# Low parts of g and of the weights on GpSimd, one scaling power for two ff tiles, w_in and w_out handled apart

## The chip, the cores and the metric

The kernel runs on one core of a Trainium2 chip. The metric is the device time of one execution in microseconds. A core has a matrix engine (TensorE, PE in the profile; its weight loads stand apart as PEld), a vector engine (VectorE, DVE), a scalar engine (ScalarE, ACT), GpSimd (POOL) and a sequencer that here issues all transfers (SyncE, SP). Each engine runs its own instructions in order; between engines, semaphores hold an instruction until what it reads is there and what it overwrites is no longer needed. SBUF is the working memory of 128 partitions; PSUM takes the matrix engine's results.

## The reference

Attention within chunks of 64 tokens, then a feed-forward layer with g(h) = h - tanh(h) between its two products. Queries, keys, values and the result are float32, the weights float64.

```python
scores = scale * np.matmul(q_c, k_c.transpose(0, 1, 2, 4, 3))   # chunks of 64, 8 batches, 8 heads
attn = np.exp(scores - np.max(scores, axis=-1, keepdims=True))
attn = attn / (np.sum(attn, axis=-1, keepdims=True) + 1e-09)
out = np.matmul(attn, v_c)
...
x = out.transpose(0, 2, 1, 3).reshape(4608, 512)
h = x @ w_in            # w_in: 512 x 2048
g = h - np.tanh(h)
return (g @ w_out).astype(np.float32)    # w_out: 2048 x 512
```

The weights come to the kernel as 64-bit words and are narrowed on the chip.

## The kernel before

**Tiling.** 4608 tokens are 36 token tiles of 128 (each a pair of chunks, called pair in the code); they go in ten groups of 4, 3, 4, 4, 4, 4, 4, 4, 3 and 2 tiles. The feed-forward layer runs group by group over 16 ff tiles of 128 columns. For one ff tile of one group, `gemm1` (L436) makes h in PSUM (`ph`), `shrink` makes g from it, and `gemm2` (L457) adds g times w_out to one PSUM bank per token tile (`po`). `gemm2` runs two ff tiles behind `gemm1` (`LAG`).

**Splitting.** A product in about float32's precision is made of three products of narrower operands: high times high, low times high, high times low. x and w_in are split into float16 parts (`xh`, `xl`, `wih`, `wil`), g and w_out into parts for the matrix engine's fp32r form (`gh`, `gl`, `woh`, `wol`). For the float16 parts the operands are first scaled by a power of two: `spread` (L94, ACT, sums of magnitudes per partition), the maximum over the partitions (L101, POOL) and three small DVE instructions (L107 to L109) give `to_w` for a tile of w_in or `to_x` for a group's x; `undo` (L422) multiplies the inverse factors, and `shrink` uses that product.

**One unit of the feed-forward layer outside PE:** tanh on ACT (L444), h - tanh on DVE (L445, from PSUM), the high part on ACT (L448), the low part gl on DVE (L449).

**A weight tile** (128 ff columns): SP loads w_in's half (L129, in four blocks) and w_out's half (L127) into one `raw` tile, three of which exist. The 64-bit words are narrowed by one ACT instruction (L139) and three on DVE (L140 shift, L144 merge of the low words, L145 sign), on both halves in one 1024-wide pass or on each half apart. Then w_in's half: spread, power, high part `wih` on ACT (L152), low part `wil` on DVE (L158); w_out's half: high part `woh` on ACT (L154), low part `wol` on DVE (L160).

**Order.** In the first stage, before and during group 0, the attention of the first seven pairs (class Early), the 16 weight tiles and group 0's feed-forward layer run interleaved. The string `PLAN` gives that order by tokens: a and v load a pair's queries, keys and values, l a weight half (l3.1 is w_out's half of tile 3), p the power of x, S M E N n T V the steps of attention, F fill matmuls without use, c a conversion, g `gemm1` and `shrink` of an ff tile (g2.1 for the second two token tiles), h a `gemm2`. Up to the bar SP and PE follow it literally; behind it a planner ranks all engines' instructions by it. Z releases the first stage's tiles, and the parts of weight tiles 8 to 15 are written where these lay. From group 1 on, the attention of the next group (class Late) is spread over the steps of the current one; its DVE instructions L316, L329, L331, L352, L359 and L366 have both inputs in SBUF, L346 and L383 one of them in PSUM.

POOL does the maximum over the partitions, and in the first stage some zero fills (L188, L290).

Of the kernel before, what the change touches and what calls it, by code (L numbers as in the profile page):

```python
# [11 lines left out]
F32 = mybir.dt.float32  # L12
# [23 lines left out]
MOST = max(SIZES) * P  # L36
LAG = 2
RAW = 3
WS = 2
EARLY_FC = 8  # L40
TINY = 2.0 ** -100
EXPONENT = 0x7F800000
# [4 lines left out]
LATE = (-1, 6, 2, 3, 3, 5, 6, 10, 10, 15)  # L47
VALS = (0, 4)
PLAN = """
a0 a1 l0.0 l0.1 a2 v2 F4 F1 v0 F4 S0 v1 v3 p0 l1.0 S1 l1.1 F1 c0 F1 a3 F6 l2.0 c1 F1 E0 N0 T0 S2 F4 l3.0 M1 M2 n1 T1 N2 V0 V1 F7 S3 T2 g0.0 M3 V2 l2.1 N3 T3 V3 | g1.0 c2 l3.1 a4 l4.0 l4.1 v4 g0.1 h c3.0 Y S4 l5.0 g2.0 a6 g3.0 E4 c3.1 h n4 a5 l5.1 c4.1 h l6.0 c4.0 l7.0 g2.1 h g3.1 v6 l6.1 h l7.1 c5 S5 E5 g1.1 g4 S6 E6 h N5 c7.0 n6 g7 c6.0 l8.0 v5 p1 T4 h T5 l8.1 V5 c7.1 c6.1 g6 T6 V4 l9.0 h V6 Z l10.0 h c8 l11.0 h l11.1 l10.1 l9.1 g5 c9 g8 g9 c10.0 h c10.1 l12.0 c11 h l13.0 l12.1 c12 g10 l14.0 h h c13.0 g11 l14.1 l15.0 h g12 l13.1 l15.1 c13.1 g13 h h c14.0 c14.1 c15 h g14 g15 h h  # L50
"""

@with_exitstack
def attn_ffn_kernel(ctx: ExitStack, tc: tile.TileContext, qE, kE, vE, qT, kT, vP, w_in, w_out, out):

# [14 lines left out]
    ps_a = ctx.enter_context(tc.tile_pool(name="ps_a", bufs=2, space=PSUM))  # L70


    wi = [[None, None] for _ in range(FC)]
    wo = [[None, None] for _ in range(FC)]

    def weight_tiles(pool, fcs):
        for fc in fcs:
            for i, a in enumerate("hl"):
                wi[fc][i] = pool.tile([P, DM], F16, name=f"wi{a}{fc}")
# [4 lines left out]
    to_w = const.tile([P, FC], F32, name="to_w")  # L84
    from_w = const.tile([P, FC], F32, name="from_w")

    def new_x():
        return tuple(xpool.tile([P, KC, MOST], F16, name=f"x{a}") for a in "hl")
# [1 line left out]
    def spread(pool, a, out):  # L90

        junk = pool.tile([P, 4 * P * 2], BF16, name="junk", bufs=1)
        n = a.shape[1]
        nc.scalar.activation(junk[:, :n], a, AF.Abs, scale=2.0 ** -10, accum_out=out)  # L94
# [20 lines left out]
        return to, back  # L115


    raws, ws, from_x = {}, {}, {}
    BOTH = slice(0, 2)

    def load_weights(pool, fc, half):
        fs = slice(fc * P, (fc + 1) * P)
        if half == 0:
            raws[fc] = pool.tile([P, 2, DM, 2], U32, name="raw", bufs=RAW)
        raw = raws[fc][:, half]
        if half:
            nc.sync.dma_start(out=raw, in_=w_out[fs])  # L127
        else:
            nc.sync.dma_start(  # L129
                out=raw.rearrange("p (kc f) two -> p kc f two", kc=KC),  # L130
                in_=w_in[:, fs, :].rearrange("(kc p) f two -> p kc f two", p=P),
            )

    def magnitude(pool, fc, part):
        up = raws[fc][:, part, :, 1]
        if fc not in ws:
            ws[fc] = pool.tile([P, 2, DM], U32, name="w", bufs=WS)
        w = ws[fc][:, part]
        nc.scalar.activation(w.bitcast(F32), up.bitcast(F32), AF.Abs, scale=2.0 ** -112)  # L139
        nc.vector.tensor_single_scalar(w, w, 3, op=ALU.logical_shift_left)  # L140

    def narrow(pool, fc, part):
        low, up, w = raws[fc][:, part, :, 0], raws[fc][:, part, :, 1], ws[fc][:, part]
        nc.vector.scalar_tensor_tensor(out=w, in0=low, scalar=29, in1=w, op0=ALU.logical_shift_right, op1=ALU.bitwise_or)  # L144
        nc.vector.scalar_tensor_tensor(out=w, in0=up, scalar=0x80000000, in1=w, op0=ALU.bitwise_and, op1=ALU.bitwise_or)  # L145
        if part in (0, BOTH):
            w = ws[fc][:, 0].bitcast(F32)
            sums = pool.tile([P, 1], F32, name="wsum", bufs=2)
            spread(pool, w, sums)
            to, back = to_w[:, fc:fc + 1], from_w[:, fc:fc + 1]  # L150
            power(pool, "w", sums, to, back)
            nc.scalar.activation(wi[fc][0], w, AF.Copy, scale=to)  # L152
        if part in (1, BOTH):
            nc.scalar.copy(out=wo[fc][0], in_=ws[fc][:, 1].bitcast(F32))  # L154

    def rest(fc, part):
        if part in (0, BOTH):
            nc.vector.scalar_tensor_tensor(out=wi[fc][1], in0=ws[fc][:, 0].bitcast(F32), scalar=to_w[:, fc:fc + 1], in1=wi[fc][0], op0=ALU.mult, op1=ALU.subtract)  # L158
        if part in (1, BOTH):
            nc.vector.tensor_sub(wo[fc][1], ws[fc][:, 1].bitcast(F32), wo[fc][0])  # L160

    def weights(pool, fc, part=BOTH):
        magnitude(pool, fc, part)
        narrow(pool, fc, part)
        rest(fc, part)


    def transposed(pool, psum, s):
# [240 lines left out]
    class FeedForward:  # L409
# [2 lines left out]

        def __init__(self, g, x):
            self.g, self.x, self.queue, self.po = g, x, [], []
            self.sig, self.known = const.tile([P, FC], F32, name="sig", bufs=2), set()

        def undo(self, fc):

            if fc not in self.known:
                some = {fc} if self.g == 0 else set(range(FC))  # L420
                fs = slice(min(some), max(some) + 1)
                nc.vector.tensor_scalar_mul(self.sig[:, fs], from_w[:, fs], from_x[self.g])  # L422
                self.known |= some
            return self.sig[:, fc:fc + 1]

        def room(self, pool, tiles):
            self.po += [pool.tile([P, DM], F32, name=f"po{t}") for t in tiles]
# [1 line left out]
        def gemm1(self, fc, t0, t1):  # L429
            cols, n = slice(t0 * P, t1 * P), (t1 - t0) * P  # L430
            x = self.x
            ph = ps_h.tile([P, MOST], F32, name="ph")[:, :n]
            k = 0
            for a, b in ((0, 0), (1, 0), (0, 1)):
                for kc in range(KC):
                    nc.tensor.matmul(ph, lhsT=wi[fc][a][:, kc * P:(kc + 1) * P], rhs=x[b][:, kc, cols], start=(k == 0), stop=(k == 3 * KC - 1))  # L436
                    k += 1
            self.ph = fc, t0, t1, n, ph

        def shrink(self):  # L440
            fc, t0, t1, n, ph = self.ph
            t = ffn.tile([P, MOST], F32, name="t", bufs=3)[:, :n]
            sig = self.undo(fc)
            nc.scalar.activation(t, ph, AF.Tanh, scale=sig)  # L444
            nc.vector.scalar_tensor_tensor(out=t, in0=ph, scalar=sig, in1=t, op0=ALU.mult, op1=ALU.subtract)  # L445
            gh = ffn.tile([P, MOST], F32R, name="gh")[:, :n]
            gl = ffn.tile([P, MOST], F32R, name="gl")[:, :n]
            nc.scalar.copy(out=gh, in_=t)  # L448
            nc.vector.tensor_sub(gl, t, gh)  # L449
            self.queue.append((fc, t0, t1, (gh, gl)))  # L450

        def gemm2(self):
# [52 lines left out]
    def step(token):  # L505

        nonlocal first_psum
        kind, n, part = re.fullmatch(r"([a-zA-Z])(\d*)\.?(\d*)", token).groups()
        n, part = int(n or 0), int(part) if part else None
        if kind == "l":  # L510
            load_weights(raw, n, part)
        elif kind == "a":
            att.load(n)
        elif kind == "v":
            att.load_values(n)
        elif kind == "p":
            from_x[n] = att.powers(range(FIRST[n], FIRST[n + 1]))
        elif kind == "F":
            for _ in range(n):
                nc.tensor.matmul(idle, lhsT=warm[:, :P], rhs=warm, start=True, stop=True)  # L520
        elif kind == "S":
            att.scores(n)
        elif kind in "ME":
            att.largest(n)
            att.exponents(n, summed=kind == "E")
        elif kind in "Nn":
            att.sums(n)
            att.normalise(n, by_head=kind == "n")
        elif kind == "T":
            att.transpose(n)  # L530
            att.weights(n)
        elif kind == "V":
            att.values(n)
            att.result(n, *((x, n) if n < SIZES[0] else (nx, n - SIZES[0])))
        elif kind == "c":
            weights(raw, n, BOTH if part is None else part)
# [76 lines left out]
```

## Time and profile before

| | us |
|---|---|
| median of three runs | 902.7 (901.23 to 904.43) |
| the profiled execution | 903.85 |
| its span in the profile | 902.1 |
| PE busy / DVE / ACT / POOL in the span | 879.1 / 635.0 / 510.5 / 20.4 |

Times in profile rows are microseconds from the span's start, unless a mean is in ns. A row of the timeline reads: start, duration, engine, line, operation, written tile <- read tiles, shapes, count, and in brackets the idle time before it and what ended that. A row of a group reads: line, engine, operation, tiles, shapes, count | busy us, mean ns of one | idle time before them and what ended it. A row of the chain reads: start, duration, engine, tile, line, count. The chain is followed back from the last instruction, at each step to what released it. Spans on POOL are rough, and a matmul's end is modelled, so that neighbouring matmul records overlap.

### The profile page before, as it was taken

How to read it: one execution, taken by the hardware profiler on the slowest of the kernel's cores; microseconds unless marked ns; L12 is line 12 of the kernel's file. 1: busy time of each engine (PE TensorE's matmuls, PEld its weight loads, DVE VectorE, ACT ScalarE, POOL GpSimd, SP SyncE). 2: the span in 40 equal slices, each digit the busy share in tenths (PEclk: the TensorE clock that was granted, in tenths of full speed). 3: DMA queues.
4: the chain of work that ended last, by engine and by line, in shares of the span. 5: the costliest groups of instructions: out<-in, count | busy, mean ns of one | idle time of the engine just before them, and what ended most of it. 6: DMA issues, size and time to landing. Idle time of an engine off the chain costs nothing.

```text
span 902.1 us, 13875 instructions
## 1 busy us (share of the span) xinstructions
PE 879.1 (97%) x4905; PEld 596.5 (66%) x4905; DVE 635.0 (70%) x1331; ACT 510.5 (57%) x1109; POOL 20.4 (2%) x44
## 2 busy tenths in 40 slices
PE   8899979999999999999999999999999999999998
PEld 6776546676566666666666666666666666677776
DVE  5896897988677767785778576857785567447332
ACT  6697666775655555555565555556564455344232
POOL 2000011000000000000000000000000000000000
PEclk8798999999999999999999999999999999999999
DMA  9772243343332322232222232323232122101100
GB/s 232 207 226 93 95 163 115 108 105 80 102 77 60 93 86 79 71 82 94 82 71 76 84 82 69 90 82 82 71 84 81 39 66 60 59 24 25 47 1 24
DMA packets 78453, 78.25 MB, mean 87 GB/s; under 512 B 36912, under 2 KB 52272, under 8 KB 78384
## 3 DMA queue, kind: packets, MB, share of 16 engines
q1 hardware_dynamic: 78384, 77.36, 30.3%
q8 instruction: 39, 0.64, 0.3%
q14 instruction: 30, 0.25, 0.1%
HBM read 60.29 MB, written 9.44 MB: 77 GB/s over the span
## 4 chain that ended last, share of the span: by engine, by line
PE 80%; DVE 8%; ACT 4%; DMA 4%; issue 2%; SPq 1%; POOL 0%; ACTq 0%; DVEq 0%
PE po L457 38%; PE ph L436 36%; PE psa L341 3%; PE psa L379 2%; PE psa L271 1%; DVE t L445 1%; ACT junk L94 1%; DVE w L144 1%; DMA raw<-w_out 1%; DMA vr<-vP 1%; DMA k<-kE 1%; DVE v16l L316 1%; DVE w L145 1%; DVE gl L449 1%; ACT t L444 1%
## 5 line engine op out<-in xcount | busy, mean ns | idle before, releaser
L457 PE MATMUL po<-woh,gh 128*128 128x512 f32 x576 | 239.4, 416 | 0.9 <-ACT gh L448 0.9
L457 PE MATMUL po<-woh,gl 128*128 128x512 f32 x576 | 227.2, 396 | 0.6 <-DVE gl L449 0.5
L457 PE MATMUL po<-wol,gh 128*128 128x512 f32 x576 | 226.0, 392 | 0.0
L436 PEld LDWEIGHTS <-wih 128*128 128x128 f16 x1312 | 117.2, 99 | 129.5 <-issue 27.3
L445 DVE SCALAR_TENSOR_TENSOR t<-ph,sig,t 128x512 f32<-128x512 f32 (+2 forms) x164 | 112.3, 685 | 111.9 <-ACT t L444 109.3
L444 ACT ACTIVATE t<-ph,sig 128x512 f32<-128x512 f32 (+2 forms) x164 | 104.2, 636 | 136.9 <-PE ph L436 127.1
L436 PE MATMUL ph<-xh,wih 128*128 128x512 f16 (+2 forms) x656 | 155.5, 361 | 8.8 <-ACT wih L152 5.2
L436 PE MATMUL ph<-xh,wil 128*128 128x512 f16 (+2 forms) x656 | 153.8, 358 | 0.7 <-DVE wil L158 0.7
L436 PE MATMUL ph<-xl,wih 128*128 128x512 f16 (+2 forms) x656 | 152.7, 356 | 0.1
L449 DVE TENSOR_TENSOR gl<-t,gh 128x512 fp32r<-128x512 f32 (+2 forms) x164 | 102.5, 625 | 64.9 <-ACT gh L448 62.4
L448 ACT CAST gh<-t 128x512 fp32r<-128x512 f32 (+2 forms) x164 | 92.6, 565 | 81.5 <-PE po L457 60.8
L457 PEld LDWEIGHTS po<-woh,gl 128*128 128x128 f32 x576 | 108.2, 188 | 27.1 <-DVE gl L449 2.9
L457 PEld LDWEIGHTS po<-woh,gh 128*128 128x128 f32 x576 | 108.8, 189 | 24.9 <-ACT gh L448 2.4
L457 PEld LDWEIGHTS po<-wol,gh 128*128 128x128 f32 x576 | 108.8, 189 | 19.0
L436 PEld LDWEIGHTS <-wil 128*128 128x128 f16 x656 | 64.3, 99 | 63.8 <-DVE wil L158 2.4
L345 ACT COPY slo<-psa 64x128 f32<-64x128 f32 x232 | 59.4, 256 | 56.6 <-DVE s L346 54.3
L346 DVE TENSOR_TENSOR s<-psa,slo 64x128 f32<-64x128 f32 x232 | 66.1, 285 | 15.6 <-ACT slo L345 12.1
L316 DVE SCALAR_TENSOR_TENSOR v16l<-vr,to_x,v16h 64x256 f16<-64x256 f32 x116 | 52.3, 478 | 19.6 <-ACT v16h L314 18.4
L341 PE MATMUL psa<-ks,qs 128*128 128x256 f32 x232 | 57.0, 326 | 2.9 <-DVE ks L331 2.7
L341 PEld LDWEIGHTS psa<-ks,qs 128*128 128x128 f32 x232 | 43.0, 189 | 17.5 <-PE ph L436 2.5
L314 ACT ACTIVATE v16h<-vr,to_x 64x512 f16<-64x512 f32 x58 | 41.7, 719 | 16.4 <-PE psa L379 15.6
L329 DVE TENSOR_TENSOR qs<-qr,qs 64x512 fp32r<-64x512 f32 x58 | 39.7, 685 | 2.4 <-ACT qs L328 1.5
(81 smaller groups left out, 762.4 us busy)
## 6 DMA issues: line engine op xcount, KB each, us to landing
qr<-qT SPq DMA_DIRECT2D x116, 128.0 KB, 2.7
kr<-kT SPq DMA_DIRECT2D x116, 128.0 KB, 2.7
out<-t SPq DMA_DIRECT2D x36, 256.0 KB, 2.3
raw<-w_in SPq DMA_DIRECT2D x16, 512.0 KB, 4.1
raw<-w_out SPq DMA_DIRECT2D x16, 512.0 KB, 5.2
vr<-vP SPq DMA_DIRECT2D x58, 128.0 KB, 2.6
qbd<-qE SPq DMA_DIRECT2D x14, 128.0 KB, 4.8
k<-kE SPq DMA_DIRECT2D x7, 256.0 KB, 5.1
```

The lines of the kernel that those rows point to most:

```text
L314: nc.scalar.activation(vh[r, :, :, r], v[r], AF.Copy, scale=to[r])
L316: nc.vector.scalar_tensor_tensor(out=vl[r, c, :, r], in0=v[r, c], scalar=to[r], in1=vh[r, c, :, r], op0=ALU.mult, op1=ALU.subtract)
L329: nc.vector.tensor_sub(qs[D:], qr[D:], qs[D:])
L341: nc.tensor.matmul(ps[:, i], lhsT=d["qs"][:, h, :], rhs=d["ks"][:, h], start=True, stop=True)
L345: nc.scalar.copy(out=slo[r], in_=ps[r, :, 1, r])
L346: nc.vector.tensor_add(d["s"][r, 2 * j:2 * j + 2, :], ps[r, :, 0, r], slo[r])
L436: nc.tensor.matmul(ph, lhsT=wi[fc][a][:, kc * P:(kc + 1) * P], rhs=x[b][:, kc, cols], start=(k == 0), stop=(k == 3 * KC - 1))
L444: nc.scalar.activation(t, ph, AF.Tanh, scale=sig)
L445: nc.vector.scalar_tensor_tensor(out=t, in0=ph, scalar=sig, in1=t, op0=ALU.mult, op1=ALU.subtract)
L448: nc.scalar.copy(out=gh, in_=t)
L449: nc.vector.tensor_sub(gl, t, gh)
L457: nc.tensor.matmul(self.po[t], lhsT=gg[a][:, ts], rhs=wo[fc][b], start=(fc == 0 and i == 0), stop=(fc == FC - 1 and i == 2))
```

## The change

- gl of every unit (L449) moves from DVE to POOL.
- Of weight tiles 2 to 15, w_out's low part moves to POOL; w_in is scaled in place on POOL, its high part is a plain ACT copy of that, and its low part a POOL subtraction. Tiles 0 and 1 stay on ACT and DVE.
- One power serves two neighbouring ff tiles: `to_w`, `from_w` and `sig` have 8 columns in place of 16; the reduction takes two columns, and one small DVE maximum is added.
- w_in and w_out have raw tiles and conversions of their own: two raw tiles for pairs of w_in tiles, three for w_out; every narrowing pass is 512 wide. w_in is laid out on the host so that a tile is one contiguous block.
- PLAN is written anew for this.

```diff
-a0 a1 l0.0 l0.1 a2 v2 F4 F1 v0 F4 S0 v1 v3 p0 l1.0 S1 l1.1 F1 c0 F1 a3 F6 l2.0 c1 F1 E0 N0 T0 S2 F4 l3.0 M1 M2 n1 T1 N2 V0 V1 F7 S3 T2 g0.0 M3 V2 l2.1 N3 T3 V3 | g1.0 c2 l3.1 a4 l4.0 l4.1 v4 g0.1 h c3.0 Y S4 l5.0 g2.0 a6 g3.0 E4 c3.1 h n4 a5 l5.1 c4.1 h l6.0 c4.0 l7.0 g2.1 h g3.1 v6 l6.1 h l7.1 c5 S5 E5 g1.1 g4 S6 E6 h N5 c7.0 n6 g7 c6.0 l8.0 v5 p1 T4 h T5 l8.1 V5 c7.1 c6.1 g6 T6 V4 l9.0 h V6 Z l10.0 h c8 l11.0 h l11.1 l10.1 l9.1 g5 c9 g8 g9 c10.0 h c10.1 l12.0 c11 h l13.0 l12.1 c12 g10 l14.0 h h c13.0 g11 l14.1 l15.0 h g12 l13.1 l15.1 c13.1 g13 h h c14.0 c14.1 c15 h g14 g15 h h
+a0 a1 l0.0 l1.0 v0 v1 a2 v2 v3 p0 F4 F1 l0.1 F4 S0 S1 l1.1 F1 a3 F6 l2.0 l3.0 E0 c0.0 c1.0 N0 T0 S2 F4 M1 M2 n1 c0.1 T1 N2 V0 V1 F7 S3 T2 l2.1 g0.0 c1.1 M3 V2 l3.1 N3 T3 V3 | g1.0 c2.0 c3.0 a4 l4.0 l5.0 v4 g0.1 h c2.1 Y S4 l4.1 l5.1 g1.1 a6 g2.0 E4 c3.1 h n4 a5 c4.0 c5.0 h l6.0 l7.0 c4.1 g3.0 h v6 g2.1 h l6.1 l7.1 c5.1 S5 E5 g3.1 h g4 S6 E6 h N5 c6.0 c7.0 n6 g5 l8.0 l9.0 v5 p1 T4 h T5 c6.1 V5 c7.1 g6 T6 V4 h V6 Z l8.1 l9.1 c8.0 c9.0 l10.0 l11.0 g7 h c8.1 g8 c9.1 h g9 l10.1 l11.1 c10.0 c11.0 h c10.1 l12.0 l13.0 c11.1 l12.1 c12.0 c13.0 g10 l13.1 h c12.1 g11 l14.0 l15.0 h g12 c13.1 l14.1 l15.1 c14.0 c15.0 h g13 c14.1 c15.1 h g14 h g15 h h h
...
         if half:
-            nc.sync.dma_start(out=raw, in_=w_out[fs])
...
+            raw_out[fc] = pool.tile([P, DM, 2], U32, name="raw_out", bufs=RAW)
+            nc.sync.dma_start(out=raw_out[fc], in_=w_out[fc])
+            return
+        j, i = divmod(fc, 2)
+        if i == 0:
+            raw_in[j] = pool.tile([P, 2, DM, 2], U32, name="raw_in", bufs=2)
+        nc.sync.dma_start(out=raw_in[j][:, i], in_=w_in[fc])
+
+    def merged(w, raw):
+        low, up = raw[:, :, 0], raw[:, :, 1]
         nc.scalar.activation(w.bitcast(F32), up.bitcast(F32), AF.Abs, scale=2.0 ** -112)
         nc.vector.tensor_single_scalar(w, w, 3, op=ALU.logical_shift_left)
...
         nc.vector.scalar_tensor_tensor(out=w, in0=low, scalar=29, in1=w, op0=ALU.logical_shift_right, op1=ALU.bitwise_or)
         nc.vector.scalar_tensor_tensor(out=w, in0=up, scalar=0x80000000, in1=w, op0=ALU.bitwise_and, op1=ALU.bitwise_or)
...
+    def weights(pool, fc, part):
+        if part:
+            w = pool.tile([P, DM], U32, name="w_out", bufs=2)
+            merged(w, raw_out.pop(fc))
+            w = w.bitcast(F32)
+            nc.scalar.copy(out=wo[fc][0], in_=w)
+            (nc.vector if fc < 2 else nc.gpsimd).tensor_sub(wo[fc][1], w, wo[fc][0])
+            return
+        j, i = divmod(fc, 2)
+        if i == 0:
+            w_in_f[j] = pool.tile([P, 2, DM], U32, name="w_in", bufs=2), pool.tile([P, 2], F32, name="wsum", bufs=2)
+        w, sums = w_in_f[j]
+        merged(w[:, i], raw_in[j][:, i])
+        w = w.bitcast(F32)
+        spread(pool, w[:, i], sums[:, i:i + 1])
+        if i == 0:
+            return
+        to = to_w[:, j:j + 1]
+        power(pool, "w", sums, to, from_w[:, j:j + 1])
+        h, l = wi[j]
+        for i in range(2):
+            if j == 0:
+                nc.scalar.activation(h[:, i], w[:, i], AF.Copy, scale=to)
+                nc.vector.scalar_tensor_tensor(out=l[:, i], in0=w[:, i], scalar=to, in1=h[:, i], op0=ALU.mult, op1=ALU.subtract)
+            else:
+                nc.gpsimd.tensor_scalar_mul(w[:, i], w[:, i], to)
+                nc.scalar.copy(out=h[:, i], in_=w[:, i])
+                nc.gpsimd.tensor_sub(l[:, i], w[:, i], h[:, i])
...
-            nc.vector.tensor_sub(gl, t, gh)
+            nc.gpsimd.tensor_sub(gl, t, gh)
...
-        "w_in": bits(inputs["moe_w_in"]),
+        "w_in": bits(inputs["moe_w_in"].reshape(KC, P, FC, P).transpose(2, 1, 0, 3)),
```

More of the change, by code (lines that the diff above doesn't have):

```diff
@@ L70, in attn_ffn_kernel @@
     ps_a = ctx.enter_context(tc.tile_pool(name="ps_a", bufs=2, space=PSUM))
-    wi = [[None, None] for _ in range(FC)]
+    wi = [[None, None] for _ in range(FC // 2)]
     wo = [[None, None] for _ in range(FC)]
@@ L78, in weight_tiles @@
             for i, a in enumerate("hl"):
-                wi[fc][i] = pool.tile([P, DM], F16, name=f"wi{a}{fc}")
+                if fc % 2 == 0:
+                    wi[fc // 2][i] = pool.tile([P, 2, DM], F16, name=f"wi{a}{fc // 2}")
                 wo[fc][i] = pool.tile([P, DM], F32R, name=f"wo{a}{fc}")
     weight_tiles(const, range(EARLY_FC))
-    to_w = const.tile([P, FC], F32, name="to_w")
-    from_w = const.tile([P, FC], F32, name="from_w")
+    to_w = const.tile([P, FC // 2], F32, name="to_w")
+    from_w = const.tile([P, FC // 2], F32, name="from_w")
     def new_x():
@@ L115, in token_power @@
         return to, back
-    raws, ws, from_x = {}, {}, {}
-    BOTH = slice(0, 2)
+    raw_in, raw_out, w_in_f, from_x = {}, {}, {}, {}
     def load_weights(pool, fc, half):
[L122 to L125, printed above, removed]
         if half:
-            nc.sync.dma_start(out=raw, in_=w_out[fs])
[L128 to L132, printed above, removed]
@@ L414, in __init__ @@
             self.g, self.x, self.queue, self.po = g, x, [], []
-            self.sig, self.known = const.tile([P, FC], F32, name="sig", bufs=2), set()
+            self.sig, self.known = const.tile([P, FC // 2], F32, name="sig", bufs=2), set()
         def undo(self, fc):
[L419 to L422, printed above, removed]
+            j = fc // 2
+            if j not in self.known:
+                some = {j} if self.g == 0 else set(range(FC // 2))
+                js = slice(min(some), max(some) + 1)
+                nc.vector.tensor_scalar_mul(self.sig[:, js], from_w[:, js], from_x[self.g])
                 self.known |= some
-            return self.sig[:, fc:fc + 1]
+            return self.sig[:, j:j + 1]
         def room(self, pool, tiles):
@@ L535, in step @@
         elif kind == "c":
-            weights(raw, n, BOTH if part is None else part)
+            for k in (0, 1) if part is None else (part,):
+                weights(raw, n, k)
         elif kind == "g":
@@ L605 @@
         if a.dtype == np.int64:
-            ap = ap.bitcast(U32).rearrange("a (b two) -> a b two", two=2)
+            ap = ap.bitcast(U32).rearrange("a b (c two) -> a b c two", two=2)
         args.append(ap)
```

30 lines of the change are left out of this document (2 added, 28 removed).

## The prediction

> **What bounds the kernel now.** I read the page's first two parts first.
>
> ```profile
> PE 879.1 (97%) x4905; PEld 596.5 (66%) x4905; DVE 635.0 (70%) x1331; ACT 510.5 (57%) x1109; POOL 20.4 (2%) x44
> PEclk8798999999999999999999999999999999999999
> ```
>
> PE is busy nearly everywhere and POOL hardly ever; the granted clock is under nine tenths only in three of the first four slices. A busy PE row counts overlapping records, so it does not say whether PE runs at its pace. For that I took the table by windows (columns: PE, PEld, DVE, ACT, POOL, clock, DMA share, GB/s) and the chain in order of time.
>
> ```profile
> 60.00:80.00 20.00, 18.80 (x106) 12.92 (x103) 16.39 (x49) 19.32 (x67) 1.43 (x4) 1.00 0.27 93
> 100.00:120.00 20.00, 15.54 (x67) 8.32 (x65) 18.85 (x37) 12.45 (x22) 2.29 (x3) 1.00 0.46 158
> 120.00:139.40 19.40, 18.21 (x75) 10.76 (x75) 18.79 (x42) 13.93 (x27) 1.05 (x3) 0.91 0.25 82
> 240.00:850.00 610.00, 609.92 (x3383) 406.79 (x3382) 424.48 (x872) 327.09 (x682) 3.47 (x6) 1.00 0.26 71
> ...
> 242.36 2.61 PE ph L436 x12
> 244.97 2.76 PE po L457 x12
> ```
>
> From 240 to 850 us PE has no gap, and the chain is PE alone: 2.61 + 2.76 = 5.37 us for one ff tile of four token tiles. Nothing on DVE, ACT or POOL can shorten that stretch. Between 100 and 139.4 us it is DVE that is full (37.64 of 39.4 us, 96%). From 60 to 80 it is ACT (19.32 of 20), so relief of DVE buys little there.
>
> What DVE's load costs PE is read from the power of each weight tile, one POOL reduction per tile. The first and the last of the eight in the second half of the weights, and the matmul that waited longest:
>
> ```profile
> 97.32 0.35 POOL L101 PARTITION_ALL_REDUCE wall<-wsum  x1 [18.24 <-ACT junk L94]
> 139.67 0.55 POOL L101 PARTITION_ALL_REDUCE wall<-wsum  x1 [5.97 <-ACT junk L94]
> 120.91 1.89 PE L436 MATMUL ph<-xh,wih 128*128 128x512 f16 x4 [4.63 <-ACT wih L152]
> ```
>
> Seven distances in 139.67 - 97.32 = 42.35 us: a weight tile comes every **6.05 us**, while PE would use one every 5.37. The 0.68 us between them, seven times, is 4.8 us; the 4.63 us gap is most of it in one place. This stretch decides the change.
>
> **The change there, part by part.** DVE's groups in the stretch from 97 to 140 us, seven tiles' worth:
>
> ```profile
> L158 DVE SCALAR_TENSOR_TENSOR wil<-w,to_w,wih 128x512 f16<-128x512 f32 x7 | 5.2, 748 | 0.0
> L445 DVE SCALAR_TENSOR_TENSOR t<-ph,sig,t 128x512 f32<-128x512 f32 x7 | 5.2, 744 | 1.2 <-ACT t L444 1.2
> L144 DVE SCALAR_TENSOR_TENSOR w<-raw,w 128x1024 uint32<-128x1024 uint32 x4 | 4.9, 1222 | 0.0
> L145 DVE SCALAR_TENSOR_TENSOR w<-raw,w 128x1024 uint32<-128x1024 uint32 x4 | 4.9, 1218 | 0.0
> L449 DVE TENSOR_TENSOR gl<-t,gh 128x512 fp32r<-128x512 f32 x7 | 4.8, 684 | 0.0
> L160 DVE TENSOR_TENSOR wol<-w,woh 128x512 fp32r<-128x512 f32 x7 | 4.8, 683 | 0.0
> L144 DVE SCALAR_TENSOR_TENSOR w<-raw,w 128x512 uint32<-128x512 uint32 x6 | 4.0, 689 | 0.1
> L145 DVE SCALAR_TENSOR_TENSOR w<-raw,w 128x512 uint32<-128x512 uint32 x6 | 4.0, 686 | 0.0
> L140 DVE TENSOR_SCALAR w<-w 128x512 uint32<-128x512 uint32 x6 | 2.5, 424 | 0.0
> L140 DVE TENSOR_SCALAR w<-w 128x1024 uint32<-128x1024 uint32 x3 | 2.1, 691 | 0.0
> L422 DVE TENSOR_SCALAR sig<-from_w,from_x 128x1 f32<-128x1 f32 x6 | 1.2, 203 | 0.0
> L109 DVE RECIPROCAL to_w<-from_w 128x1 f32<-128x1 f32 x7 | 1.1, 158 | 0.1
> L107 DVE TENSOR_SCALAR wall<-wall 128x1 uint32<-128x1 uint32 x7 | 1.1, 154 | 1.8 <-POOL wall L101 1.8
> L108 DVE TENSOR_SCALAR from_w<-wall 128x1 f32<-128x1 f32 x7 | 1.0, 148 | 0.1
> ```
>
> They add up to 46.8 us, 6.69 per tile; set against 6.05, an instruction overlaps its neighbour so that 0.905 of its duration counts.
>
> DVE loses L158, L160 and L449 (0.748 + 0.683 + 0.684 = 2.12 us) and half of the power and of sig. It pays for the split of the halves: two 512-wide passes, 2 x (0.424 + 0.689 + 0.686) = 3.60 us, where the joint form took 0.691 + 1.222 + 1.218 = 3.13. The power of a pair has one more small reduction (taken as 0.154, like L107): (0.158 + 0.154 + 0.148 + 0.154) / 2 = 0.31. With sig 0.10 and L445 0.744 that is 4.75, times 0.905 = **4.30 us** of DVE's own work per tile, below PE's 5.37. Were DVE alone to decide, PE would set the pace: -0.68 x 7 = -4.8 us.
>
> POOL gets three subtractions (low parts of g, w_in, w_out; price X each), one scaling (price Y) and half a reduction (0.18 of the 0.35). The trace holds no POOL instruction with two inputs. The nearest row is a pass of 512 columns that only writes:
>
> ```profile
> L188 POOL MEMSET qbd<- 64x512 f32 x4 | 2.1, 520 | 0.2
> ```
>
> X is at least one such pass, 0.52, and at most three, one after the other, 1.56. I take two, **X = 1.04**, since two operands have to come in; Y = 0.52, one operand (at most 1.04, which would add 0.52 x 7 = 3.6 us). POOL's own load is then 3 x 1.04 + 0.52 + 0.18 = 3.82 us per tile, under 5.37: POOL alone sets no pace.
>
> **What POOL and DVE do to each other** is the open price. Three pairs from the timeline, POOL's reduction and the DVE instruction that was running when it began:
>
> ```profile
> 115.98 1.23 DVE L144 SCALAR_TENSOR_TENSOR w<-raw,w 128x1024 uint32<-128x1024 uint32 x1
> 116.07 1.34 POOL L101 PARTITION_ALL_REDUCE wall<-wsum  x1 [7.27 <-ACT junk L94]
> ...
> 107.90 0.68 DVE L449 TENSOR_TENSOR gl<-t,gh 128x512 fp32r<-128x512 f32 x1
> 108.20 0.60 POOL L101 PARTITION_ALL_REDUCE wall<-wsum  x1 [5.43 <-ACT junk L94]
> ...
> 133.05 0.75 DVE L445 SCALAR_TENSOR_TENSOR t<-ph,sig,t 128x512 f32<-128x512 f32 x1
> 133.35 0.35 POOL L101 PARTITION_ALL_REDUCE wall<-wsum  x1 [5.71 <-ACT junk L94]
> ```
>
> Beside L445, which has one operand in PSUM, the reduction takes 0.35 us. Beside L144 it takes 1.34 and ends 0.20 after it (117.41 against 117.21); beside L449 it takes 0.60 and ends 0.22 after it. Both have two SBUF inputs: POOL stood until DVE was through. That DVE stands while POOL reads is not shown. Either DVE does not, and the pace is PE's, or it does, and the two engines' instructions of this sort follow one another.
>
> In the second case DVE's merge passes (L140, L144, L145), 3.60 x 0.905 = 3.26 us per tile, and POOL's 3.82 share one lane: 7.08 us per tile, 1.03 more than now, times 7: **+7.2 us**. At X = 0.52 it is 5.52 per tile, -3.7 us; at X = 1.56 it is 8.64, +18.1 us. It breaks even at X = (6.05 - 3.26 - 0.70) / 3 = 0.70. I take the second case, because the one direction that is seen is a full stand and not a slowdown, and because 7.08 is further from 6.05 than a little overlap takes away. I count L140 in the lane: 512 more columns cost it 0.267 us, L144 0.533, so it draws two columns at once.
>
> The Trainium skill, "SBUF — State Buffer", section "Who interferes with whom", states that a VectorE instruction with two SBUF inputs and a GpSimd instruction that reads SBUF hold one shared pair of ports in turn, each for its whole length, whichever starts first; the POOL side of it agrees with the 1.34 us above, and the other side no row here shows. Its page "GPSIMD Engine Reference", section "Elementwise — side-by-side cycle accounting", gives 4497 ns for an add of 2048 columns; a quarter, 1.12 us (an estimate), in place of 1.04 would make the lane 7.32 and the term +8.9.
>
> **The other parts.** Start: the first real matmul waits for x, whose power came from POOL at 26.34.
>
> ```profile
> 26.34 0.38 POOL L101 PARTITION_ALL_REDUCE xall<-vsum  x1 [5.98 <-ACT junk L94]
> 28.90 1.01 PE L436 MATMUL ph<-xh,wih 128*128 128x256 f16 x4 [2.00 <-ACT xh L278]
> ```
>
> The new order puts the same bytes ahead of the last value tile (w_in of tile 1 where w_out of tile 0 was), and ACT's work ahead of x stays about even: one more spread and one more wih, one woh and the joint L139 of tile 1 less. Tile 1's weights are then there with tile 0's, which saves a later wait, but the conversions of w_out move behind it. -1 us, between -3 and +2.
>
> The transfers: w_in becomes one block per tile, and raw tiles are kept apart.
>
> ```profile
> SPq L129 <- DVE w L145: 74.5, 12, 18.3
> ```
>
> SP's loads of w_in wait for a free raw tile, 74.5 us in sum, so a load that lands faster is behind that wait: 0. SP gets no more transfers of weights, and what stands behind a waiting load on SP (values and keys of the next group) waits on the same merges as now.
>
> Groups 1 and 2: here DVE prepares attention ahead, and PE lacks a little.
>
> ```profile
> 160.00:180.00 20.00, 18.52 (x100) 13.01 (x98) 19.03 (x42) 14.68 (x35) 0.00 (x0) 1.00 0.41 115
> 220.00:240.00 20.00, 18.03 (x103) 10.91 (x101) 13.37 (x30) 12.50 (x27) 0.00 (x0) 1.00 0.27 79
> ```
>
> PE lacks 1.48 + 1.97 = 3.5 us in these two. DVE loses sixteen subtractions of 384 columns, at three quarters of 0.684 some 8.2 us; in the lane POOL's sixteen (0.78 each, 12.5 us) give back what meets a two-input DVE instruction, about half. -2 us, between -4 (all of the gap and a little more) and +3 (all of the 12.5 given back).
>
> Steady groups: gl takes X + up to one DVE instruction (1.7 us) in place of 0.68 and is read two ff tiles later, 2 x 5.37 us; the cover is PE's own work, so 0. Were the cover gone, 0.36 us a tile would show. In POOL's order the subtraction of w_in's low part waits for ACT's copy; the next gl and the next power stand behind it, and PE's second product behind gl: within the same two tiles. Tail: the chain's last product run (18 matmuls, three ff tiles), and the last gl.
>
> ```profile
> 895.36 0.42 DVE L449 TENSOR_TENSOR gl<-t,gh 128x256 fp32r<-128x256 f32 x1 [0.60 <-ACT gh L448]
> ...
> 893.73 4.12 PE po L457 x18
> ```
>
> The last ff tile's third begins 2.75 us into that run, at 896.48; its gl was done at 895.78 and may come 0.70 later, more than a 256-wide POOL pass adds (half of 1.04 against 0.42). 0.
>
> **Sum**, against the profiled execution (903.85 us, its span 902.1): +7.2 - 1 - 2 = +4.2, so 908.0 there. The median of the three runs, 902.7, is 1.15 below that execution; for the median I say **906.9**.
>
> **The rivals.**
> *DVE never stands for POOL (faster).* It decides if POOL's hold on the lane costs DVE under 1.75 us a tile (6.05 - 4.30). For it: only POOL is seen to stand, DVE drops from 6.05 to 4.30. Against: the full stand of 1.34. Price: -4.8 - 1 - 4 = -9.8, 892.9; some 2.5 us more if the stretch at half clock (84.52, twelve matmuls in 5.07 us in place of 2.61) goes too.
>
> ```profile
> 84.52 5.07 PE ph L436 x12
> ```
>
> *POOL is dear.* X near 1.56: +18.1 - 1 + 3 = +20.1, 922.8. For it: no two-input row at all; against: a pass that writes 0.52 is quick.
> *The lane fills, but earlier work pays.* Before 97.32 POOL sat 18.24 us and DVE was not full; if the in-halves of one pair are merged in that hole, 2 x 1.80 x 0.905 = 3.3 us leave the stretch: +4.2 - 3.3 = +0.9, 903.6, no change. Against: its raw tiles come free late.
>
> **How the numbers follow.** Chances: forecast 0.42 (own range 901 to 913), no standing 0.35, dear POOL 0.10, paid earlier 0.13. A measurement of this kernel tells about 0.3% (2.7 us) from no change. Slower: 0.28 of the forecast's 0.42, all 0.10, 0.03 of the fourth: 0.41. Same: 0.11 + 0.02 + 0.08 = 0.21. Faster: 0.03 + 0.33 + 0.02 = 0.38. Range **888 to 916**: it takes in the case without standing with part of its 2.5, and stops short of dear POOL.
>
> **What would show it.** In the changed profile: DVE instructions with two SBUF inputs that last over a microsecond or idle behind POOL, and a spacing of pairs near 2 x 7.1 us between 97 us and the end of the weights, would show the lane; two-input DVE rows unchanged at 0.68 beside POOL's, and pairs every 10.7 us, would show it wrong. POOL's row of gl gives X. Past 240 us the chain should stay PE's at 5.37 a tile; if not, the cover was wrong and so is the sum.

## The result and the profile after

| | before | after |
|---|---|---|
| median, us | 902.16 (901.23 to 904.43) | 1022.74 (1020.40 to 1024.72) |
| ratio | | 1.1331 (1.1293 to 1.1370) |
| span of the profiled execution | 902.1 | 1022.8 |

The change costs 120.6 us. A small loss was forecast, 4.2 us; the sign is as forecast, the size is nearly thirty times the forecast's. The profile's page of after, first two parts:

```profile
PE 919.0 (90%) x4903; PEld 608.6 (60%) x4903; DVE 578.4 (57%) x1142; ACT 512.5 (50%) x1118; POOL 267.9 (26%) x242
...
PEclk9876957779999999999999999999999999999999
```

DVE's busy time fell by 56.6 us, as the change meant it to, and no engine looks like the bound: POOL, the only one whose share of the span grew, is at 26%. The low clock digits now reach to the ninth slice (230 us) instead of the fourth. So the page says where to look, and not why. Here are windows of after in that stretch (columns as in the prediction: PE, PEld, DVE, ACT, POOL, clock, DMA share, GB/s):

```profile
140.00:160.00 20.00, 9.19 (x29) 3.55 (x28) 6.86 (x13) 5.04 (x9) 9.68 (x7) 0.66 0.07 20
160.00:180.00 20.00, 7.28 (x21) 3.16 (x20) 5.88 (x12) 5.71 (x12) 9.87 (x9) 0.68 0.10 35
...
240.00:850.00 610.00, 586.25 (x3204) 383.36 (x3202) 398.69 (x790) 332.63 (x703) 137.66 (x111) 0.99 0.28 78
```

In these 40 us of the first stage nobody is busy: PE under half, DVE a third, POOL half, and the granted clock is at 0.66 and 0.68. Past 240 us, where its first stage ends, PE lacks 23.75 of 610 us. Before it lacked 0.08 of these, and 4.2 of the 88.5 us from its own stage's end (151.5) to 240. Both halves of the forecast are therefore to be explained, the first stage and the "0" of the steady groups.

How much belongs to which half is read from the transfers of the result: group 0's first one marks the end of the first stage, the last one the end of the work. The groups of transfers, of before and of after (last two numbers: first and last start):

```profile
L484 SPq DMA_DIRECT2D out<-t x36: 332/344/1541, 151.5 to 898.6; - x36
```

```profile
L484 SPq DMA_DIRECT2D out<-t x36: 332/344/1667, 240.9 to 1019.8; - x36
```

The first stage takes 89.4 us more, all that follows 31.8 more (778.9 against 747.1).

What everybody waits for is seen on POOL's timeline in that stage. One full pair of w_in tiles of after, and the reduction that opens the next:

```profile
139.37 0.37 POOL L101 PARTITION_ALL_REDUCE wall<-wsum  x1 [5.76 <-issue]
147.15 1.25 POOL L449 TENSOR_TENSOR gl<-t,gh 128x512 fp32r<-128x512 f32 x1 [7.40 <-issue]
148.40 3.12 POOL L162 TENSOR_SCALAR w_in<-w_in,to_w 128x512 f32<-128x512 f32 x2
151.50 1.25 POOL L143 TENSOR_TENSOR wol<-w_out,woh 128x512 fp32r<-128x512 f32 x1
152.72 2.44 POOL L164 TENSOR_TENSOR wil<-w_in,wih 128x512 f16<-128x512 f32 x2
155.12 1.71 POOL L143 TENSOR_TENSOR wol<-w_out,woh 128x512 fp32r<-128x512 f32 x1
162.57 0.57 POOL L101 PARTITION_ALL_REDUCE wall<-wsum  x1 [5.74 <-issue]
170.70 2.49 POOL L449 TENSOR_TENSOR gl<-t,gh 128x512 fp32r<-128x512 f32 x2 [7.56 <-issue]
```

The reader is to look at the brackets. No other engine is named as a releaser here: each idle stretch is put down to "issue", to nothing that the profile shows. Nor was data missing ahead of the reduction at 162.57, for ACT had its sums done by 121 us. 5.74 us stand ahead of a reduction, 7.40 and 7.56 behind one, and none between subtractions and scalings. The pair takes 162.57 - 139.37 = 23.2 us, 11.6 per ff tile where 6.05 was the pace before; some 10 us of it are work, and for 13.1 POOL stands still. That engine is the bound of this stage, and its busy share does not show it. The other engines hang on it, PE and ACT of after:

```profile
172.00 1.65 PE L457 MATMUL po<-woh,gl 128*128 128x512 f32 x3 [8.68 <-POOL gl L449]
...
174.78 0.62 ACT L163 CAST wih<-w_in 128x512 f16<-128x512 f32 x1 [10.55 <-POOL w_in L162]
```

A hint of what POOL does in the gaps stands in the records of its sequencer at the reduction's line, of before and of after:

```profile
L101 POOLq MODIFY_POOL_CONFIG  x2: 4/4/4, 13.8 to 13.8; - x2
```

```profile
L101 POOLq MODIFY_POOL_CONFIG  x34: 1/8/13, 5.9 to 795.7; - x34
```

These records say that POOL's configuration is changed for the reduction, so it and the elementwise instructions appear not to run from the same program. Before had 26 reductions and two such records in all, at the start; after has 18 reductions, the first two (19.55 and 24.08 us) with nothing between, and 34 records: two for each of the 17 times that POOL comes to the reduction from other work. The way back leaves no record at this line. The Trainium skill, "GPSIMD Engine Reference", section "Instruction dispatch", states that the first call of a freshly loaded program costs POOL about 6 us with no instruction in the profile; the 5.74 us ahead of a reduction agrees. That the way back takes 7.4 us more, and that mixed kinds pay at every turn, is what these rows suggest and experiments 1 and 2 test.

The same happens once per group later on. POOL of after around one power of x, PE at that place, and PE's waits between 240 and 850 us (sum, times, longest):

```profile
385.29 1.26 POOL L449 TENSOR_TENSOR gl<-t,gh 128x512 fp32r<-128x512 f32 x1 [5.49 <-ACT gh L448]
392.93 0.67 POOL L101 PARTITION_ALL_REDUCE xall<-vsum  x1 [6.38 <-PE ph L436]
400.78 2.50 POOL L449 TENSOR_TENSOR gl<-t,gh 128x512 fp32r<-128x512 f32 x2 [7.18 <-DVE s L351]
```

```profile
402.09 0.76 PE L457 MATMUL po<-woh,gl 128*128 128x512 f32 x2 [2.10 <-POOL gl L449]
```

```profile
PE po L457 <- POOL gl L449: 15.4, 7, 3.6
PE psa L340 <- DVE ks L330: 2.6, 3, 1.2
```

The last gl before the power ends at 386.55, the next begins at 400.78: 14.2 us without one, where the cover is two ff tiles, 10.7 us. PE runs dry behind it, here for 2.10 us, and 15.4 us of the 23.75 that it lacks are such waits. The brackets of POOL name PE and DVE as releasers, but the lengths, 6.38 and 7.18 us, are those of the stretches called "issue" above: so I take it that the named instruction merely ended last.

### The profile page after: what moved, and what is told of

Its sections match the earlier page's. It is cut to its first block, busy times and chain, and to the rows that moved or that the text cites. A ratio compares the mean times of both kernels' runs of the same rounds, so it can differ in the third digit from the quotient of the medians.

```text
span 1022.8 us, 14197 instructions
## 1 busy us (share of the span) xinstructions
PE 919.0 (90%) x4903; PEld 608.6 (60%) x4903; DVE 578.4 (57%) x1142; ACT 512.5 (50%) x1118; POOL 267.9 (26%) x242
## 3 DMA queue, kind: packets, MB, share of 16 engines
q1 hardware_dynamic: 72240, 77.36, 26.5%
## 4 chain that ended last, share of the span: by engine, by line
PE 71%; DVE 6%; POOL 5%; issue 5%; ACT 3%; DMA 2%; SPq 0%; ACTq 0%; POOLq 0%; DVEq 0%
PE po L457 35%; PE ph L436 32%; PE psa L340 2%; POOL gl L449 2%; POOL w_in L162 2%; PE psa L378 2%; DVE t L445 1%; DMA out<-t 1%; POOL wil L164 1%; POOL wol L143 1%; DVE qs L328 1%; DVE s L345 1%; ACT ks L329 0%; ACT t L444 0%; DVE mx L350 0%
## 5 line engine op out<-in xcount | busy, mean ns | idle before, releaser
L449 POOL TENSOR_TENSOR gl<-t,gh 128x512 fp32r<-128x512 f32 (+2 forms) x164 | 194.0, 1185 | 615.0 <-ACT gh L448 492.3
L457 PE MATMUL po<-woh,gl 128*128 128x512 f32 x576 | 232.9, 412 | 58.5 <-POOL gl L449 58.4
L457 PE MATMUL po<-woh,gh 128*128 128x512 f32 x576 | 242.4, 422 | 2.5 <-ACT gh L448 2.5
L457 PE MATMUL po<-wol,gh 128*128 128x512 f32 x576 | 230.5, 400 | 4.4 <-POOL wol L143 4.4
L436 PE MATMUL ph<-xh,wih 128*128 128x512 f16 (+2 forms) x656 | 162.1, 372 | 9.3 <-ACT wih L163 4.8
L457 PEld LDWEIGHTS po<-woh,gl 128*128 128x128 f32 x576 | 110.6, 195 | 91.6 <-POOL gl L449 66.6
L436 PE MATMUL ph<-xh,wil 128*128 128x512 f16 (+2 forms) x656 | 157.4, 364 | 8.0 <-POOL wil L164 8.0
L436 PE MATMUL ph<-xl,wih 128*128 128x512 f16 (+2 forms) x656 | 157.0, 363 | 0.0
L315 DVE SCALAR_TENSOR_TENSOR v16l<-vr,to_x,v16h 64x256 f16<-64x256 f32 x116 | 59.3, 539 | 30.7 <-ACT v16h L313 29.5
L330 DVE TENSOR_TENSOR ks<-kr,ks 128x512 fp32r<-128x512 f32 x58 | 49.1, 847 | 19.6 <-ACT ks L329 19.5
L340 PEld LDWEIGHTS psa<-ks,qs 128*128 128x128 f32 x232 | 42.2, 189 | 22.5 <-issue 7.2
```

The source lines that it names most:

```text
L315: nc.vector.scalar_tensor_tensor(out=vl[r, c, :, r], in0=v[r, c], scalar=to[r], in1=vh[r, c, :, r], op0=ALU.mult, op1=ALU.subtract)
L330: nc.vector.tensor_sub(ks[:, :, 1, :], kr, ks[:, :, 0, :])
L340: nc.tensor.matmul(ps[:, i], lhsT=d["qs"][:, h, :], rhs=d["ks"][:, h], start=True, stop=True)
L436: nc.tensor.matmul(ph, lhsT=wi[fc // 2][a][:, fc % 2, kc * P:(kc + 1) * P], rhs=x[b][:, kc, cols], start=(k == 0), stop=(k == 3 * KC - 1))
L449: nc.gpsimd.tensor_sub(gl, t, gh)
L457: nc.tensor.matmul(self.po[t], lhsT=gg[a][:, ts], rhs=wo[fc][b], start=(fc == 0 and i == 0), stop=(fc == FC - 1 and i == 2))
```

## The experiments

The theories: **S**, the changes of program on POOL; **L**, the lane of the prediction, with POOL and DVE standing for each other and POOL's own length; later **C**, the way of w_in alone, which goes from the power through POOL's scaling, ACT's copy and POOL's subtraction before `gemm1` may begin. Each run has its before beside it on the same chip.

**1. No reduction on POOL.** In the changed kernel a copy on DVE stands where the reduction was:

```diff
-        nc.gpsimd.partition_all_reduce(al, sums, channels=P, reduce_op=bass_isa.ReduceOp.max)
+        nc.vector.tensor_copy(al, sums)
```

> The changed kernel with every reduction over the partitions on POOL replaced by a small DVE copy (the power is then each partition's own, not the largest of all); everything else, all of POOL's elementwise work among it, stays. Theory S (POOL changes its program between the reduction and an elementwise instruction, 6 to 8 us each way, 33 more times than before): no change of program is left, so 100 to 120 us go and the time is 900 to 920. Theory L (POOL's elementwise instructions are long, and DVE and POOL stand for one another): the time stays above 1000.

935.39 us, ratio 1.0353 (1.0327 to 1.0379): 31.9 over its before. Of the 120.6 us, 88.7 go with the changes of program, and in them whatever a reduction waits in line behind POOL's subtractions, which isn't told apart. The time lies outside both theories' ranges. Its transfers and its windows later on:

```profile
L484 SPq DMA_DIRECT2D out<-t x36: 332/340/1372, 179.5 to 927.2; - x36
```

```profile
240.00:850.00 610.00, 608.34 (x3348) 400.92 (x3347) 399.46 (x776) 329.83 (x689) 138.33 (x108) 1.00 0.27 74
```

Behind the first stage it takes 747.7 us, as before did (747.1), and PE lacks 1.7 of 610 us, with every gl on POOL. So the cover of two ff tiles holds for gl; what broke it was the change of program. The rest, 28.0 us, lies in the first stage.

**2. Changes of program without any load.** In the kernel before, one addition of a single column behind each reduction, whose result nothing reads:

```diff
         nc.gpsimd.partition_all_reduce(al, sums, channels=P, reduce_op=bass_isa.ReduceOp.max)
+        tiny = pool.tile([P, 1], F32, name="tiny", bufs=2)
+        nc.gpsimd.tensor_add(tiny, sums[:, 0:1], sums[:, 0:1])
```

> The kernel before with one [128,1] addition on POOL behind each of its 26 reductions, of which nobody reads the result: next to no load, no lane taken. Theory S: each reduction now has a change of program before and behind it; the 18 in the first stage are each some 6 to 14 us late, of which part is hidden: 930 to 1010. Theory L: 902 to 905.

1035.61 us, ratio 1.1470 (1.1444 to 1.1496): 132.2 us for 26 instructions. Its POOL timeline and its records:

```profile
126.85 0.38 POOL L101 PARTITION_ALL_REDUCE wall<-wsum  x1 [6.45 <-issue]
134.47 0.18 POOL L103 TENSOR_TENSOR tiny<-wsum 128x1 f32<-128x1 f32 x1 [7.25 <-issue]
141.87 0.38 POOL L101 PARTITION_ALL_REDUCE wall<-wsum  x1 [7.21 <-issue]
```

```profile
L101 POOLq MODIFY_POOL_CONFIG  x52: 1/4/11, 13.6 to 800.7; - x52
```

52 records for 26 reductions, and 15.0 us from one power to the next (141.87 - 126.85) where the instructions take 0.56. Some 0.8 us of the 15 go by while ACT makes the next sums, which can begin only when the addition has read the old ones. Theory S is shown by itself, and larger than its own upper number. The first transfer of the result comes at 282.3 us, 130.8 late, and all behind it takes 748.6 us: later on nothing waits for the tiny instruction, and there the changes cost nothing.

**3 and 4. Everything but POOL's new work; gl alone.** The changed kernel with each elementwise instruction back on DVE and the weights scaled on ACT as before (reductions stay on POOL); and the kernel before with gl on POOL:

```diff
-            (nc.vector if fc < 2 else nc.gpsimd).tensor_sub(wo[fc][1], w, wo[fc][0])
+            nc.vector.tensor_sub(wo[fc][1], w, wo[fc][0])
...
-            if j == 0:
+            if True:
...
-            nc.gpsimd.tensor_sub(gl, t, gh)
+            nc.vector.tensor_sub(gl, t, gh)
```

```diff
-            nc.vector.tensor_sub(gl, t, gh)
+            nc.gpsimd.tensor_sub(gl, t, gh)
```

> The changed kernel with every subtraction and scaling taken off POOL again (gl, wol and wil on DVE, the scaling in ACT's copy): what is left is one power for two tiles, weights in and out apart, the layout and the new order. Theories S and L: both put the whole loss on POOL's work, so 893 to 915. If more than 950, the loss is in the new order or the pairs, and both fall.

> The kernel before with gl alone on POOL. Theory S: 26 reductions, most with gl on both sides, so up to 50 changes of program, more in the first stage than in the changed kernel (16 powers of weights in place of 8): 980 to 1080. Theory L: POOL has 19 us of work per group and no weights, so the first stage gains or loses little: 895 to 910.

910.00 us, ratio 1.0079 (1.0052 to 1.0107), and 1017.93 us, ratio 1.1230 (1.1154 to 1.1306). The new order, the pairs and the split weights cost 6.6 us themselves, 4.4 of it behind the first stage; gl alone, in the old order and beside 26 reductions, costs 114.5 us, nearly as much as the whole change. Theory S had both runs, theory L only the first.

**5 to 8. Parts of the elementwise work without changes of program.** All four are experiment 1 with more put back: the weights on POOL and gl on DVE; gl on POOL and the weights on DVE and ACT; nothing on POOL; and experiment 1 with the ten reductions of x on POOL again:

```diff
+        if name == "w":
+            nc.vector.tensor_copy(al, sums)
+        else:
+            nc.gpsimd.partition_all_reduce(al, sums, channels=P, reduce_op=bass_isa.ReduceOp.max)
```

> As e1_no_reduction (no reduction on POOL), with gl back on DVE: POOL keeps the low parts and the scaling of the weights alone. e1 is 935, of which the first stage has 28 us more than e3_no_pool. Theory D (POOL's own length decides: 1.9 for the scaling, 1.3 each for wil and wol, 4.5 us of POOL a tile against PE's 5.37, with DVE standing for it): most of the 28 us stays, 920 to 935. If gl is what hurts, 905 to 915.

> As e1_no_reduction, with the weights' low parts and scaling back on DVE and ACT: POOL has gl alone, 1.3 us a tile, and no change of program. Theory D: POOL is far from full, DVE is relieved of gl: 902 to 912. If gl is what hurts, 920 to 935.

> As e3_no_pool (nothing elementwise on POOL), and no reduction either: the control for e1, e5 and e6, and the price of the reduction itself where no program changes. Each reduction is 0.35 us in a chain that is mostly covered: 904 to 911.

> As e1_no_reduction, but with the ten reductions for x on POOL again (one a group, two of them in the first stage), the eight for the weights still left out. Theory S: the later groups lose what they lose in the changed kernel, 30 us over e1's (773.8 against 744.0 from the end of group 0), and the first stage two visits of some 13 us, partly covered: 965 to 985. If the changes of program cost only in the first stage: 935 to 950.

| | us | ratio to before | first transfer | from first to last |
|---|---|---|---|---|
| weights on POOL | 931.65 | 1.0320 (1.0295 to 1.0346) | 181.9 | 745.6 |
| gl on POOL | 912.25 | 1.0115 (1.0087 to 1.0143) | 154.6 | 751.8 |
| nothing on POOL | 906.86 | 1.0047 (1.0032 to 1.0062) | 154.2 | 748.2 |
| experiment 1 and x's reductions | 970.75 | 1.0756 (1.0720 to 1.0792) | 192.0 | 770.2 |

Against "nothing", gl costs 5.4 us and the weights 24.8. Experiment 1, which has both, is 31.9 - 4.5 = 27.4 above it (each less its own before), a little under their sum. The ten reductions of x bring 68.4 - 31.9 = 36.5 us: 12.5 in the first stage and 22.5 later, as S has it for one turn per group. The eight of the weights then bring the other 52 of the 88.7.

**9. The power by a matmul.** The kernel before; the powers of tiles 2 to 15 and of group 1's x come from a 128 x 128 matmul (a mean in place of the maximum), so that POOL has no reduction there, and wol of these tiles goes to POOL; beside it the same with wol on DVE:

```diff
+            tot = ps_a.tile([P, n], F32, name="psa")
+            nc.tensor.matmul(tot, lhsT=mean, rhs=sums, start=True, stop=True)
+            nc.vector.tensor_copy(al, tot)
...
-            nc.vector.tensor_sub(wo[fc][1], ws[fc][:, 1].bitcast(F32), wo[fc][0])
+            (nc.gpsimd if fc > 1 else nc.vector).tensor_sub(wo[fc][1], ws[fc][:, 1].bitcast(F32), wo[fc][0])
```

> The kernel before, with the powers of weight tiles 2 to 15 and of group 1's x made without POOL (the mean over the partitions, times a fixed power of two, by a [128,128] matmul of a constant, and not the maximum), and w_out's low part of these tiles on POOL, so that no reduction stands between POOL's subtractions. DVE loses 0.68 of 6.69 us a tile and gains back what it stands for POOL, at most 1.25 a tile; PE waits a little at each of the 15 small products: 896 to 912.

> Its control: the same powers by matmul, w_out's low part on DVE as before. 902 to 910: the product's wait on PE is the only thing that changes.

908.73 us, ratio 1.0068 (1.0045 to 1.0091), and 909.50 us, ratio 1.0066 (1.0039 to 1.0092). DVE's relief by fourteen wol is worth nothing that can be told here, and the matmul's way costs some 6 us. This was meant to be faster than both kernels, and it is not faster than before.

**10 and 11. Which of the weights' steps.** Experiment 7 with wol alone on POOL, and with w_in's scaling and low part alone:

```diff
-            nc.vector.tensor_sub(wo[fc][1], w, wo[fc][0])
+            (nc.vector if fc < 2 else nc.gpsimd).tensor_sub(wo[fc][1], w, wo[fc][0])
```

```diff
-            if True:
+            if j == 0:
```

> As e7_none (906.9), with one thing on POOL: the low part of w_out for tiles 2 to 15, no reductions. e5 showed that the weights cost 25 us on POOL and e6 that gl costs 5. Theory C (it is the chain of w_in that hurts: power, two scalings on POOL, ACT's copy, two subtractions on POOL, and then the product that waits for them): w_out's low part is needed two ff tiles later, so 902 to 911. Theory W (any weight work on POOL hurts by its length and by DVE standing): half of the 25, 915 to 922.

> The other half: as e7_none, with the scaling and the low part of w_in on POOL, w_out's low part on DVE. Theory C: nearly all of the 25 us, 922 to 932. Theory W: 912 to 920.

908.24 us, ratio 1.0060 (1.0041 to 1.0080), and 927.25 us, ratio 1.0276 (1.0251 to 1.0301). wol costs 1.1 us over "nothing", which the intervals can't tell from none; w_in costs 20.1. Both times are where C had them and not where a price for any work on POOL would put them: a tile of w_in, for which ACT and DVE needed one instruction each (wih, wil), now takes three in a row over two engines (scaling, copy, subtraction), and a pair's two scalings stand ahead of its subtractions. One pair of the eleventh experiment:

```profile
126.53 5.26 POOL L162 TENSOR_SCALAR w_in<-w_in,to_w 128x512 f32<-128x512 f32 x2 [9.13 <-DVE to_w L109]
...
130.28 0.62 ACT L163 CAST wih<-w_in 128x512 f16<-128x512 f32 x1 [3.28 <-POOL w_in L162]
130.96 1.04 PE L436 MATMUL ph<-xh,wih 128*128 128x512 f16 x4 [2.93 <-ACT wih L163]
131.76 2.26 POOL L164 TENSOR_TENSOR wil<-w_in,wih 128x512 f16<-128x512 f32 x2
...
132.97 1.89 PE L436 MATMUL ph<-xh,wil 128*128 128x512 f16 x4 [0.97 <-POOL wil L164]
132.99 1.58 DVE L143 TENSOR_TENSOR wol<-w_out,woh 128x512 fp32r<-128x512 f32 x1 [4.17 <-ACT woh L142]
```

PE waits at both ends of POOL's steps, 2.93 and 0.97 us. How much of the 20 us is the row of steps, how much the length of POOL's own instructions, and how much is standing beside DVE (5.26 us here for two scalings that took 3.12 in after) was not tried apart.

## Why the prediction went wrong

**The step that failed** is the sentence "POOL's own load is then 3 x 1.04 + 0.52 + 0.18 = 3.82 us per tile, under 5.37: POOL alone sets no pace." Half a reduction was put at 0.18 us. With a change of program on either side it is (0.37 + 7.40 + 5.74) / 2, some 6.8 us per tile, and POOL's round takes 11.6. The price of an instruction that the trace of before didn't hold was bounded by its own length; what lies between it and a neighbour of another kind wasn't asked. None of the rivals had it either. What misled was a row that looked like a proof. After the reduction at 139.67 us before's POOL went on:

```profile
140.08 1.02 POOL L290 MEMSET v16h<- 128x1024 f16 x1
...
153.54 0.38 POOL L101 PARTITION_ALL_REDUCE xall<-vsum  x1 [9.77 <-ACT junk L94]
```

A zero fill follows the reduction without a gap, and there are no further records of a change. So a fill pays nothing behind a reduction; a subtraction does.

**The lane.** The forecast case, that DVE stands for POOL as POOL for DVE, is what runs show. Even so, without any change of program the time, 935.39 us, lies above the range's 916: the lane was not the whole of the rest. Groups of experiment 1: s, a DVE instruction of the attention with one input in PSUM, and ks, with both in SBUF; then the same two of before, where their lines are one higher:

```profile
L345 DVE TENSOR_TENSOR s<-psa,slo 64x128 f32<-64x128 f32 x232 | 66.4, 286 | 44.7 <-ACT slo L344 41.6
...
L330 DVE TENSOR_TENSOR ks<-kr,ks 128x512 fp32r<-128x512 f32 x58 | 51.2, 883 | 18.0 <-ACT ks L329 18.0
```

```profile
L346 DVE TENSOR_TENSOR s<-psa,slo 64x128 f32<-64x128 f32 x232 | 66.1, 285 | 15.6 <-ACT slo L345 12.1
...
L331 DVE TENSOR_TENSOR ks<-kr,ks 128x512 fp32r<-128x512 f32 x58 | 39.3, 677 | 0.1
```

883 ns against 677 for ks, 286 against 285 for s (experiments 6 and 7, which differ in gl alone, have the same 883 and 677 for ks): the rule of the Trainium skill, "SBUF — State Buffer", section "Who interferes with whom", holds in both directions, and the rival "DVE never stands" is out. The pace came out near the one worked out, but by luck. Powers of experiment 1, from DVE's timeline:

```profile
111.52 0.15 DVE L101 COPY wall<-wsum 128x2 f32<-128x2 f32 x1
...
138.15 1.23 DVE L101 COPY wall<-wsum 128x2 f32<-128x2 f32 x1
...
152.98 1.22 DVE L101 COPY wall<-wsum 128x2 f32<-128x2 f32 x1
```

Six tiles in 41.46 us are 6.91 per tile, where 7.08 was worked out. With X = 1.25 and Y = 1.56, as measured below, the same sum gives 3.26 + 3 x 1.25 + 1.56 = 8.57 (8.15 with the four gl that POOL ran there instead of six): two prices too small made up for a sum that let nothing of the two engines' work overlap. Nor does the pace follow that sum from run to run. Experiment 11 has only w_in's steps on POOL, and its same three distances take 153.54 - 108.56 = 44.98 us, 7.50 per tile. With nothing on POOL, experiment 7:

```profile
102.35 0.16 DVE L101 COPY wall<-wsum 128x2 f32<-128x2 f32 x1
...
137.45 0.40 DVE L101 COPY wall<-wsum 128x2 f32<-128x2 f32 x1
```

5.85 per tile. POOL's elementwise work costs 41.46 - 35.10 = 6.4 us over these six tiles (forecast for the lane: 7.2 over seven); the runs don't show how much of it is the lane. But the fifth power is 9.2 us late already (111.52 against 102.35), and from the last power to the first transfer it takes 26.5 us (179.5 - 152.98) instead of 16.8 (154.2 - 137.45). These 18.9 us, outside the stretch in which the sum was made, are the second error: POOL's work was priced where DVE was full, and not ahead of it and at its end. In experiment 11 the fifth power is 6.2 us late and the end only 2.0 longer (172.3 - 153.54 = 18.8), so w_in's longer way explains most of the first and little of the second by itself.

**X and Y.** Undisturbed, gl takes 1.25 us; the groups of after, gl and the scaling, also hold what they stand:

```profile
L449 POOL TENSOR_TENSOR gl<-t,gh 128x512 fp32r<-128x512 f32 x108 | 142.3, 1320 | 442.8 <-ACT gh L448 351.8 <-issue 43.6 <-DVE s L351 29.1
...
L162 POOL TENSOR_SCALAR w_in<-w_in,to_w 128x512 f32<-128x512 f32 x14 | 21.9, 1561 | 0.0
```

X was taken as 1.04, within bounds of 0.52 to 1.56: off by a fifth; the estimate of 1.12 in the prediction, worked out from the Trainium skill, "GPSIMD Engine Reference", section "Elementwise — side-by-side cycle accounting", is nearer. Y was taken as 0.52, at most 1.04; it is 1.56. The scaling, with one operand fewer, is not cheaper than a subtraction but dearer by 0.31. With both, POOL's own load is 3 x 1.25 + 1.56 = 5.31 us per tile even without a reduction, just under PE's 5.37.

**Start** (-1): the first feed-forward matmul of after begins at 35.88 us and not before 28.90, though x's power is ready earlier (24.08). On PE the same attention steps stand ahead of it in both orders, but they end later: ACT copies the second `aT` at 26.18 us instead of 20.17, behind the sums of v and both wih, and PE waits 2.86 us for it. With the elementwise work off POOL (experiment 3) the first transfer comes at 151.4 us against 151.5, so the stage ends as before, and nothing is won.

**Groups 1 and 2** (-2): nothing of it is seen; experiment 1 takes 747.7 us behind the first stage, before 747.1. **Steady groups** (0): right for gl without changes of program, wrong with them, as the prediction said would show the cover gone: 15.4 us of PE's waits there are for gl, about half of the 31.8, and experiment 8 puts 22.5 of it on x's reductions. **Tail** (0): right, the chain of after ends with a run of 18 products of the same length, as before's did:

```profile
1014.90 4.12 PE po L457 x18
```

**The change's own frame** (pairs, order, split weights) was priced into these terms at a gain or nothing; it costs 4.5 us without any reduction on POOL and 6.6 with them, which their intervals don't tell apart. Which piece of it does that wasn't tried apart.

**The sum as measured**, each less its own before: 4.5 for the frame, 27.4 for all elementwise work on POOL (alone: gl 5.4, w_in 20.1, wol 1.1) and 88.7 for the changes of program make the 120.6 us. (The last two are differences of runs, so they add up by construction; the tests are experiments 2 and 8.) All three were priced at +4.2 together, and the largest at 0.18 us a tile.

## What to carry to other kernels

Before work is moved to GpSimd, see what else runs there: a reduction over partitions and elementwise instructions in turn cost some 13 us of standing for each round in this kernel. Keeping that engine to one kind removed it here, though the elementwise work still cost its own time (experiment 1); grouping the kinds to have fewer rounds was not tried. An engine at 26% busy can be the bound; look at its timeline for idle stretches whose releaser is "issue" and whose lengths repeat. And when a price has no row, bound not only the instruction but what stands between it and its neighbours.

## What was not expected of the hardware

- POOL's change of program, in the rows shown: 5.7 to 6.5 us ahead of a reduction, counted from when its sums are there, and 7.2 to 7.6 behind it, also for an instruction of 0.18 us (experiment 2). It is recorded at the sequencer and isn't counted as busy.
- A zero fill on POOL behind a reduction needs no such change; a one-input scaling by a value per partition is slower there (1.56 us) than a two-input subtraction (1.25).
- A one-input DVE instruction stands for POOL as well, as the prediction took it for L140, and for longer than one POOL instruction. POOL of after runs three subtractions without a gap from 177.50 to 180.99 us; the shift of one half that began beside them, and the next one, undisturbed:

```profile
178.26 3.01 DVE L133 TENSOR_SCALAR w_out<-w_out 128x512 uint32<-128x512 uint32 x1 [13.94 <-ACT w_out L132]
...
181.92 0.42 DVE L133 TENSOR_SCALAR w_in<-w_in 128x512 uint32<-128x512 uint32 x1
```
